# Sliding-window attention beside a gated MLP: P times V in two row tiles of 64 keys

## The chip, the cores and the metric

The kernel runs on one core of one Trainium2 chip. The metric is the device time of one execution in microseconds (us), as the median of several runs. The core's engines are TensorE (PE in the profile; PEld is its weight load), VectorE (DVE), ScalarE (ACT), GpSimd (POOL) and SyncE (SP), which issues the DMAs.

## What is computed

x has 2048 rows of 640. The result is x plus two branches of the same normalized x: causal attention in a sliding window, and a gated MLP. Cut from the reference:

```python
H = 32; Dh = D // H; W = 256                       # D = 640, so Dh = 20
q, k, v = split heads of (xn @ wqkv)
scores = einsum("bhqd,bhkd->bhqk", q, k) * (Dh ** -0.5)
mask = (idx[:, None] - idx[None, :] >= 0) & (idx[:, None] - idx[None, :] < W)
p = softmax(where(mask, scores, -1e9))
A = einsum("bhqk,bhkd->bhqd", p, v) -> (S, D) @ wo
B = (sigmoid(xn @ w_gate) * (xn @ w_up)) @ w_down  # F = 1536
return x + A + B                                   # xn = layernorm(x)
```

A query at position i sees the keys i - 255 to i: one diagonal piece, full pieces, and one oldest piece.

## The kernel before

The 2048 rows are worked in four chunks of 512 (`c` = 0 to 3). For each chunk the kernel normalizes x (`g_norms`; from chunk 1 on the reciprocal standard deviation `rstds` is made on POOL, L269 and L270, and the rows are scaled on DVE, L275), turns it so that features lie on partitions (`xnT`), and projects q, k and v (`proj_block` L302, `project_v` L330). q and k go through a scratch in DRAM (`st` to `sq`, `sk`, L310) and come back spread out (`spread`, L318), so that the 20 features of each head start at a partition divisible by 32. Four heads (`i` = 0 to 3) make a group; there are eight groups. v stays on chip with its keys on partitions: 21 columns per head, the last of them 0.5, which makes PV produce half the softmax denominator beside the output.

Attention goes in steps, listed by `steps_of` and run by `scores` (L485): a step fills one tile `ps` of 128 partitions x 4 heads x 512 columns in PSUM, ACT takes its exp into `pT` (L490), and POOL zeroes what the mask excludes (`affine_select`, here called a select, L493). A unit is 64 queries or 64 keys (`U`). In the step, partitions are 128 keys and columns are queries; the two halves of 64 keys are separate matmuls (`hf`), which write the two halves of the partitions. Each matmul has 20 rows and 64 columns of the array, at one of four row groups and two column halves. For chunks 1 to 3 a group has two wide steps (diagonal, full and oldest pieces, three selects each), and two groups share one full step, which has no select. Chunk 0 has two wide steps per group. That makes 16 steps in chunk 0 and 20 in each other chunk: 76.

`pv` (L519) then multiplies P by V for one group: each matmul takes 128 keys, the four heads write the four 32-partition strips of the accumulator `acc`, and the pieces of all steps accumulate. `finish_group` turns the accumulator on DVE (L529), `scale_group` divides (L537, L541) and turns it back to `oc` (L545).

The order of the work is written out by hand (`manual_schedule`): each engine runs its instructions in the order of the program. The main loop runs the 76 steps in order; after each step it pulls dense work out of a list (`Fill`): the projections of the next chunk, the MLP's gate and up matmuls (L412, L419, with tanh on ACT in L415 and the product `h` on DVE in L423), and the output rows (down projection L433, `wo` L440, row addition on DVE L444). How much is pulled is given by estimated costs, spread evenly over the steps up to a due time. P times V of a group is due one step after the last step of its pair (two in chunk 0), so that at that step both groups of the pair run `pv` one after the other, then the step's scores follow. Accumulators (`pg`, `pu`, `pqk`, `pv`, `y`, `acc`) share four PSUM slots in rotation; `ps` has one buffer (four banks), `pT` five.

Of the kernel before, what the change touches and what calls it, by code (L numbers as in the profile page):

```python
# [43 lines left out]
PTW = 10 * U  # L44

SPAN = 5


def wide_step(g, r, old):  # L60

    q = 2 * r
    if old:
        return dict(scores=[(g, 0, r, q, 5, 1), (g, 1, r, q + 1, 5, 2), (g, 0, r + 2, q + 4, 2, 6),
                            (g, 1, r - 2, q, 2, 0), (g, 0, r - 2, q, 1, 0), (g, 1, r + 2, q + 5, 1, 7)],
                    late=(1, 8, 2), diag=1, oldest=(0, 2),
                    pv=[(g, r, q, 5, 1), (g, r + 2, q + 4, 2, 6), (g, r, q + 5, 1, 9),
                        (g, r - 2, q, 2, 0, 8)])

    scores = [(g, 0, r, q, 5, 0), (g, 1, r, q, 6, 0)]  # L70
    if r == 0:
        scores += [(g, 0, 2, 4, 3, 5), (g, 1, 2, 5, 2, 6)]
        last = [(g, 2, 4, 3, 5)]
    else:
        scores += [(g, 0, 3, 6, 2, 5), (g, 1, 3, 7, 1, 6), (g, 0, 2, 7, 1, 7), (g, 1, 2, 7, 1, 7)]
        last = [(g, 3, 6, 2, 5), (g, 2, 7, 1, 7)]
    return dict(scores=scores, late=(5, 9, 1), diag=0, oldest=(4, 1),
                pv=[(g, r, q, 5, 0), (g, r, q + 5, 1, 9)] + last)


def full_step(gs):

    pieces = [(g, r, q, 2, 4 * n + col) for n, g in enumerate(gs) for r, q, col in ((-1, 0, 0), (2, 6, 2))]
    return dict(scores=[(g, hf, *rest) for g, *rest in pieces for hf in range(2)], pv=pieces)


def steps_of(c):
    if c == 0:
        return [wide_step(g, r, False) for g in range(NG) for r in range(2)]
    out = []  # L90
    for g in range(0, NG, 2):
        out += [wide_step(g + k, r, True) for k in range(2) for r in range(2)]
        out.append(full_step((g, g + 1)))
    return out
# [13 lines left out]
def kernel(  # L108
# [115 lines left out]
    def turn_wo():  # L224
        for i in range(HG):
            nc.sync.dma_start(out=wo_i[i].rearrange("(g d) n -> g d n", d=DH),
                              in_=A_wo.rearrange("(g i d) n -> i g d n", i=HG, d=DH)[i])
# [62 lines left out]


    qk = {}
    vt = {}

    def proj_block(w, c, m):

# [408 lines left out]
    for t, (c, _, step) in enumerate(todo):  # L705
        for piece in step["pv"]:
            ends[c, piece[0]] = t
# [96 lines left out]
```

## Time and profile before

| what | value |
|---|---|
| median of 3 runs | 312.26 us (312.17 to 312.5) |
| profiled execution, span from first to last instruction | 310.6 us |
| what lies around the span (median less span) | 1.66 us |
| granted TensorE clock, mean | 1.000 |
| instructions in the profile | 10139 |
| scores L485, PE | 1856 matmuls |
| P times V L519, PE | 1184 matmuls |
| selects L493, POOL | 192, 146.8 us busy |
| exp L490, ACT | 76, 142.7 us busy, 1878 ns each |

The profile lists busy time by engine, the span in 40 slices, the chain of work that ended last, groups of instructions by line, operation and tile, and the DMAs. A busy PE is not PE at its peak, as matmuls overlap; start times in the timeline show its pace.

### The profile page before, as it was taken

Reading aid. Unit: us, or ns where it says so; the run is one execution under the profiler, and the core shown is the slowest. Engines: PE = TensorE matmul, PEld = TensorE weight load, DVE = VectorE, ACT = ScalarE, POOL = GpSimd, SP = SyncE. Lnnn points to the kernel's source line nnn. Section 1 sums busy time; section 2 is a strip of 40 time slices with the busy share of each in tenths; the row PEclk is TensorE's granted clock in tenths of the full one; section 3 lists DMA queues with packets and bytes.
Section 4 is the critical chain, followed back from the end, with each engine's and each line's share of the span. In section 5 each row is a group of like instructions: output and inputs, shape, how many; then the busy total and the mean of one; then the engine's idle time right before and its main releaser. Section 6 shows DMA issues by size and latency. Waiting matters only on the chain.

```text
span 310.6 us, 10139 instructions
## 1 busy us (share of the span) xinstructions
PE 303.6 (98%) x4436; PEld 175.0 (56%) x4471; DVE 159.0 (51%) x313; ACT 192.5 (62%) x179; POOL 155.4 (50%) x239
## 2 busy tenths in 40 slices
PE   7999999999999999999999999999999999999996
PEld 3654444556557655644567665644546675454775
DVE  5533655639775154289826155272733526272423
ACT  6623878697763747787673647767585547768000
POOL 3000675676782827567382637546273846656000
PEclk9999999999999999999999999999999999999999
DMA  7997999765534153440035212450000220000302
GB/s 219 367 298 253 321 182 318 258 185 170 177 65 108 44 160 100 164 151 2 2 44 87 88 59 88 154 190 2 2 3 2 66 64 23 2 2 2 88 22 65
DMA packets 40301, 35.69 MB, mean 115 GB/s; under 512 B 10400, under 2 KB 39712, under 8 KB 40224
## 3 DMA queue, kind: packets, MB, share of 16 engines
q1 hardware_dynamic: 39392, 34.27, 37.6%
q10 hardware_dynamic: 864, 0.77, 0.9%
q8 instruction: 35, 0.57, 0.8%
q14 instruction: 10, 0.08, 0.1%
HBM read 23.63 MB, written 10.26 MB: 109 GB/s over the span
## 4 chain that ended last, share of the span: by engine, by line
PE 96%; issue 1%; DMA 1%; ACT 1%; DVE 0%; SPq 0%
PE y L433 17%; PE pu L419 17%; PE pg L412 17%; PE pqk L302 14%; PE ps L485 9%; PE pv L330 7%; PE y L440 7%; PE acc L519 7%; DMA xc<-in_A_x_dram 1%; PE pt L282 0%; ACT xn L614 0%; ACT xn L619 0%; DVE xn L625 0%; SPq L171 0%; ACT rstd L620 0%
## 5 line engine op out<-in xcount | busy, mean ns | idle before, releaser
L493 POOL TENSOR_SCALAR_AFFINE_SELECT pT<-pT 128x512 bf16<-128x512 bf16 (+2 forms) x192 | 146.8, 795 | 128.3 <-ACT pT L490 128.1
L490 ACT ACTIVATE pT<-ps 128x2048 bf16<-128x2048 f32 x76 | 142.7, 1878 | 64.3 <-PE ps L485 59.4
L423 DVE SCALAR_TENSOR_TENSOR h<-th,pu 128x512 bf16<-128x512 f32 x48 | 32.7, 683 | 58.2 <-PE pu L419 43.6
L419 PE MATMUL pu<-xnT,wu 128*128 128x512 bf16 x228 | 59.2, 380 | 0.7
L412 PE MATMUL pg<-xnT,wg 128*128 128x512 bf16 x226 | 58.0, 380 | 0.9 <-issue 0.5
L433 PE MATMUL y<-wd,h 128*128 128x320 bf16 (+2 forms) x396 | 57.0, 295 | 0.0
L302 PE MATMUL pqk<-xnT,wqkv 128*128 128x512 bf16 x191 | 45.7, 381 | 0.7 <-issue 0.2
L433 PEld LDWEIGHTS <-h 128*128 128x128 bf16 x396 | 36.6, 98 | 14.4
L415 ACT ACTIVATE th<-pg 128x512 f32<-128x512 f32 x48 | 28.6, 596 | 14.4 <-PE pg L412 14.0
L412 PEld LDWEIGHTS <-wg 128*128 128x128 bf16 x240 | 22.2, 98 | 25.2 <-issue 0.2
L419 PEld LDWEIGHTS <-wu 128*128 128x128 bf16 x240 | 21.9, 98 | 25.4 <-issue 0.6
L485 PEld LDWEIGHTS <-kT 20*64 20x64 bf16 x1856 | 20.6, 103 | 24.2 <-issue 22.3
L302 PEld LDWEIGHTS <-wqkv 128*128 128x128 bf16 x200 | 22.5, 119 | 18.4 <-issue 1.0
L529 DVE STREAM_TRANSPOSE t<-acc 128x512 f32<-128x512 f32 x32 | 21.8, 709 | 21.5 <-PE acc L519 21.2
L444 DVE SCALAR_TENSOR_TENSOR rows<-y,rows 128x320 bf16<-128x320 f32 x30 | 14.5, 490 | 35.2 <-PE y L440 30.2
L485 PE MATMUL ps<-qT,kT 20*64 20x128 bf16 (+4 forms) x1856 | 32.5, 239 | 0.0
L541 DVE TENSOR_TENSOR on<-t,rec 128x320 bf16<-128x320 f32 (+4 forms) x48 | 27.1, 565 | 1.1
L440 PE MATMUL y<-wo,oc 128*128 128x320 bf16 (+2 forms) x165 | 24.2, 295 | 0.0
L330 PE MATMUL pv<-wqkv,xnT 128*128 128x320 bf16 x160 | 23.7, 299 | 0.0
L519 PE MATMUL acc<-pT,v 128*32 128x128 bf16 (+3 forms) x1184 | 22.9, 231 | 0.0
L519 PEld LDWEIGHTS <-v 128*32 128x32 bf16 x1184 | 18.5, 97 | 7.5 <-issue 2.2
L440 PEld LDWEIGHTS <-oc 128*128 128x128 bf16 x165 | 15.5, 98 | 5.9
(45 smaller groups left out, 132.2 us busy)
## 6 DMA issues: line engine op xcount, KB each, us to landing
qT<-sq SPq DMA_DIRECT2D x7, 512.0 KB, 4.3
sq<-st SPq DMA_DIRECT2D x20, 128.0 KB, 3.6
sk<-st SPq DMA_DIRECT2D x20, 128.0 KB, 4.1
out_dram<-rows SPq DMA_DIRECT2D x15, 160.0 KB, 1.8
kT<-sk SPq DMA_DIRECT2D x4, 512.0 KB, 7.4
wg<-in_B_w_gate_dram SPq DMA_DIRECT2D x4, 480.0 KB, 7.1
wu<-in_B_w_up_dram SPq DMA_DIRECT2D x4, 480.0 KB, 6.1
xc<-in_A_x_dram SPq DMA_DIRECT2D x3, 640.0 KB, 5.5
```

The lines of the kernel that those rows point to most:

```text
L302: nc.tensor.matmul(ps, lhsT=wt[:, m, :], rhs=xnT[c][:, d, :], start=(d == 0), stop=(d == DC - 1))
L330: nc.tensor.matmul(ps[:, 0:HALF], lhsT=xnT[c][:, d, s * P:(s + 1) * P], rhs=wqkv[:, d, 2 * D + hf * HALF:2 * D + (hf + 1) * HALF], start=( ...
L412: nc.tensor.matmul(pg, lhsT=part(wg, d, f), rhs=xnT[c][:, d, :], start=(d == 0), stop=(d == DC - 1))
L415: nc.scalar.activation(out=th, in_=pg, func=TANH, scale=0.5)
L419: nc.tensor.matmul(pu, lhsT=part(wu, d, f), rhs=xnT[c][:, d, :], start=(d == 0), stop=(d == DC - 1))
L423: nc.vector.scalar_tensor_tensor(out=h, in0=th, scalar=1.0, in1=pu, op0=ADD, op1=MULT)
L433: nc.tensor.matmul(y[:, 0:cut[1] - cut[0]], lhsT=ht[c, f][:, s * P:(s + 1) * P], rhs=wd[:, f, cut[0]:cut[1]], start=(f == 0), stop=False)
L440: nc.tensor.matmul(y[:, 0:cut[1] - cut[0]], lhsT=oc[c, m][:, s * P:(s + 1) * P], rhs=wo[:, m, cut[0]:cut[1]], start=False, stop=(m == DC - 1))
L485: nc.tensor.matmul(ps[hf * U:(hf + 1) * U, i, col * U:(col + n) * U], lhsT=qk["k", kc, g // GH][32 * i:32 * i + DH, g % GH, key:key + U], ...
L490: nc.scalar.activation(out=pt[:, :, 0:CW], in_=ps, func=EXP, scale=SCALE)
L493: nc.gpsimd.affine_select(out=out, in_=in_, pattern=[[0, HG], [0, n], [sign, width]], compare_op=GE, fill=0.0, base=base, channel_multipli ...
L519: nc.tensor.matmul(acc[32 * i:32 * i + 32, q * U:(q + n) * U], lhsT=v[:, h * VW:h * VW + 32], rhs=cols[:, i, col:col + (n - 1) * by + 1:by ...
```

## The change

Two groups now share each step, one on each half of the partitions. `ps` and `pT` hold 64 keys on 64 partitions, for the first group of the pair on partitions 0 to 63 and for the second on 64 to 127. A step is a list of pieces `(u, q, n, col)`: the 64 keys of unit u, against n units of queries from unit q, in the columns from col. Chunk 0 has four steps per pair and the other chunks five, so there are 16 and 20 steps as before. Each piece is eight matmuls: two groups times four heads. Selects are made for each half of the partitions by itself: 264 instead of 192. For chunks 1 to 3 the five steps of a pair have 8, 4, 2, 2 and 2 of them.

`pv` runs both groups of the pair interleaved into two accumulators. Each matmul takes 64 keys in 64 rows of the array. Pieces are ordered by falling width. For half of the units the keys of V lie on the other half of the partitions, so each block of V gets a second tile `vx`, in which the halves are exchanged by two DMAs of 64 partitions x 347 elements (`swap_v`), issued on SP after the block's V is copied.

A pair is now made of group q of heads 0 to 15 and group q of heads 16 to 31. `spread` reads the scratch accordingly, two groups per DMA; `turn_wo` reorders wo accordingly, with eight DMAs instead of four; V is kept in two halves of 16 heads. The order of dense work is unchanged, and so are the places of the 76 steps and of the 16 places at which P times V runs.

```diff
...
+COLS = 8
+SPAN = 4
+VS = H // 2 * VW + 11
+def steps_of(c):
+    if c == 0:
+        plans = [([(6, 6, 2, 0), (0, 4, 1, 2), (1, 5, 1, 3), (7, 7, 1, 4), (2, 6, 1, 6), (3, 7, 1, 7)],
+                  (0,), (2, 3), [(6, 7, 1, 5)]),
+                 ([(4, 4, 4, 0), (5, 5, 3, 4)], (0,), (), [(5, 7, 1, 7)])]
     else:
+        plans = [([(6, 6, 2, 0), (0, 4, 1, 2), (1, 5, 1, 3), (7, 7, 1, 4), (2, 6, 1, 5), (3, 7, 1, 6), (-4, 0, 1, 7)],
+                  (0,), (2, 3, (5,)), []),
+                 ([(4, 4, 4, 0), (5, 5, 3, 4), (-3, 1, 1, 7)], (0,), ((7,),), []),
+                 ([(-1, 0, 4, 0), (-3, 0, 1, 4), (-2, 0, 3, 5)], (), (3,), [])]
+    plans += [([(u, u, 4, 0), (u + 1, u + 1, 4, 4)], (0,), (), []) for u in (0, 2)]
+    return [dict(pair=g, pv=pv, scores=pv + spare, diag=diag, oldest=oldest)
+            for g in range(0, NG, 2) for pv, diag, oldest, spare in plans]
...
     def turn_wo():
         for i in range(HG):
-            nc.sync.dma_start(out=wo_i[i].rearrange("(g d) n -> g d n", d=DH),
-                              in_=A_wo.rearrange("(g i d) n -> i g d n", i=HG, d=DH)[i])
+            for b in range(2):
+                nc.sync.dma_start(
+                    out=wo_i[i].rearrange("(q b d) n -> b q d n", b=2, d=DH)[b],
+                    in_=A_wo.rearrange("(b q i d) n -> i b q d n", b=2, i=HG, d=DH)[i, b])
...
-        src = scratch[w, c % 2].rearrange("(g p) s -> p g s", p=P)
-        nc.sync.dma_start(out=qk[w, c, half][:, first:first + g1 - g0, :], in_=src[:, g0:g1, :])
+        src = scratch[w, c % 2].rearrange("(b q p) s -> p q b s", b=2, p=P)
+        dst = qk[w, c, half][:, first:first + g1 - g0, :].rearrange("p (q b) s -> p q b s", b=2)
+        for k in range((g1 - g0) // 2):
+            nc.sync.dma_start(out=dst[:, k], in_=src[:, g0 // 2 + k])

     def new_v(c, s):
-        v = vp.tile([P, H * VW + 11], BF16, name="v")
+        v = vp.tile([P, 2, VS], BF16, name="v")
         vt[c * SBC + s] = v
-        nc.gpsimd.memset(v[:, 0:H * VW].rearrange("p (h d) -> p h d", d=VW)[:, :, DH:VW], 0.5)
-        nc.gpsimd.memset(v[:, H * VW:], 0.0)
+        nc.gpsimd.memset(v[:, :, 0:VS - 11].rearrange("p a (h d) -> p a h d", d=VW)[:, :, :, DH:VW], 0.5)
+        nc.gpsimd.memset(v[:, :, VS - 11:], 0.0)
+
+    def swap_v(c, s):
+
+        v, x = vt[c * SBC + s], vp.tile([P, VS], BF16, name="vx")
+        vx[c * SBC + s] = x
+        nc.sync.dma_start(out=x[0:U, :], in_=v[U:P, 0, :])
+        nc.sync.dma_start(out=x[U:P, :], in_=v[0:U, 1, :])
...
-        v3 = vt[c * SBC + s][:, 0:H * VW].rearrange("p (h d) -> p h d", d=VW)
-        copy(out=v3[:, hf * 16:(hf + 1) * 16, 0:DH],
+        v3 = vt[c * SBC + s][:, hf, 0:VS - 11].rearrange("p (h d) -> p h d", d=VW)
+        copy(out=v3[:, :, 0:DH],
              in_=ps[:, 0:HALF].rearrange("p (h d) -> p h d", d=DH))
...
             spread("q", c, 0, 2)
-            spread("k", c, 0, 1)
-            spread("k", c, 1, 3)
+            spread("k", c, 0, 2)
+            spread("k", c, 2, 4)
             spread("q", c, 2, 4)
-            spread("k", c, 3, 4)
+            for s in range(SBC):
+                swap_v(c, s)

     def g_v(c):
         for s in range(SBC):
             new_v(c, s)
             for hf in range(2):
                 proj_v(c, s, hf, nc.scalar.copy if hf else nc.vector.tensor_copy)
+            swap_v(c, s)
...
+        pt = pp.tile([P, HG, COLS * U], BF16, name="pT")
+        ps = ps_s.tile([P, HG, COLS * U], FP32, name="ps")
+        for u, q, n, col in step["scores"]:
+            kc, key = divmod(c * CW + u * U, CW)
+            for b in range(2):
+                g = step["pair"] + b
+                for i in range(HG):
+                    nc.tensor.matmul(
+                        ps[b * U:(b + 1) * U, i, col * U:(col + n) * U],
+                        lhsT=qk["k", kc, g // GH][32 * i:32 * i + DH, g % GH, key:key + U],
+                        rhs=qk["q", c, g // GH][32 * i:32 * i + DH, g % GH, q * U:(q + n) * U],
+                        start=True, stop=True)
+        nc.scalar.activation(out=pt, in_=ps, func=EXP, scale=SCALE)
+        cols = pt.rearrange("p h (n u) -> p h n u", u=U)
+        both = pt.rearrange("p h (a n u) -> p (h a) n u", n=SPAN, u=U)
+        for at, base, sign in [(x, 0, 1) for x in step["diag"]] + [(x, -1, -1) for x in step["oldest"]]:
+            for b in range(2):
+                rows = slice(b * U, (b + 1) * U)
+                live = cols[rows, :, at[0], :] if isinstance(at, tuple) else both[rows, :, at, :]
+                nc.gpsimd.affine_select(out=live, in_=live, pattern=[[0, live.shape[1]], [sign, U]],
+                                        compare_op=GE, fill=0.0, base=base, channel_multiplier=-sign)
         return pt

+    def pv(c, pair, made):
+        accs = [ps_d.tile([P, CW], FP32, name="acc", tag="d") for _ in range(2)]
+        flat = sorted(((piece, pt) for step, pt in made for piece in step["pv"]), key=lambda x: -x[0][2])
+        for k, ((u, q, n, col), pt) in enumerate(flat):
+            block = (c * CW + u * U) // P
+            for b in range(2):
+                rows = slice(b * U, (b + 1) * U)
+                v = vt[block][rows, b, :] if u % 2 == b else vx[block][rows, :]
+                for i in range(HG):
+                    h = (pair // 2 * HG + i) * VW
+                    nc.tensor.matmul(
+                        accs[b][32 * i:32 * i + 32, q * U:(q + n) * U],
+                        lhsT=v[:, h:h + 32], rhs=pt[rows, i, col * U:(col + n) * U],
+                        start=(k == 0), stop=(k == len(flat) - 1), skip_group_check=True)
+        for b in range(2):
+            finish_group(c, pair + b, accs[b])

...
+    ends = {(c, step["pair"]): t for t, (c, _, step) in enumerate(todo)}
+    due = {t + (1 if c else 2): (c, pair) for (c, pair), t in ends.items()}
+    cuts = [(ends[n, NG - 2] + 2 + n, f"out{n}") for n in range(NCH - 1)] + [(len(todo), None)]
...
+            n, pair = due[t]
+            fill.hurry = pair == NG - 2
+            pv(n, pair, parts.pop((n, pair)))
+            if pair == NG - 2:
+                fill.shut.discard(f"out{n}")
+        parts.setdefault((c, step["pair"]), []).append((step, scores(c, step)))
```

## The prediction

> **What bounds the kernel now.** I read the page from the top: busy shares, slices, the chain. Then groups with shapes kept apart, then timelines of two places.
>
> ```profile
> PE 303.6 (98%) x4436; PEld 175.0 (56%) x4471; DVE 159.0 (51%) x313; ACT 192.5 (62%) x179; POOL 155.4 (50%) x239
> ...
> PE   7999999999999999999999999999999999999996
> ...
> PEclk9999999999999999999999999999999999999999
> ...
> q8 instruction: 35, 0.57, 0.8%
> ...
> PE 96%; issue 1%; DMA 1%; ACT 1%; DVE 0%; SPq 0%
> PE y L433 17%; PE pu L419 17%; PE pg L412 17%; PE pqk L302 14%; PE ps L485 9%; PE pv L330 7%; PE y L440 7%; PE acc L519 7%; DMA xc<-in_A_x_dram 1%; PE pt L282 0%; ACT xn L614 0%; ACT xn L619 0%; DVE xn L625 0%; SPq L171 0%; ACT rstd L620 0%
> ```
>
> TensorE works from the second slice to the last at the full clock and is 96% of the chain. No other engine is near its limit, so time moves only if TensorE's stream gets shorter or is made to wait. Of that stream the change touches scores (L485, 9%) and PV (L519, 7% of 310.6, 21.7 us); the order of everything else on PE, DVE and ACT is the same in both programs.
>
> The stream's pace comes from start times. Dense matmuls of 512 columns start 216 ns apart, of 320 columns 136 ns: columns / 2.4 + 2.5 ns. The scores' and PV's small matmuls start 3 to 5 ns apart when they lie on different tiles of the array, and the next wave on the same tiles follows after the same columns / 2.4 + 2.5 (136 ns for 320, 56 for 128, 28 for 64). So a burst costs the columns per tile, plus 2.5 ns a wave, plus some 0.1 us at each change of tile shape: in one PV burst 80 matmuls take 1.44 us to the next matmul's start, against 3072 / 2.4 + 20 x 2.5 = 1.33.
>
> ```profile
> 109.62 0.43 PE L485 MATMUL ps<-qT,kT 20*64 20x128 bf16 x32
> 109.98 2.35 PE L302 MATMUL pqk<-xnT,wqkv 128*128 128x512 bf16 x10
> 112.27 1.51 PE L519 MATMUL acc<-pT,v 128*32 128x320 bf16 x80
> 113.71 0.43 PE L485 MATMUL ps<-qT,kT 20*64 20x320 bf16 x24
> ```
> ```profile
> 110.21 1.88 ACT L490 ACTIVATE pT<-ps 128x2048 bf16<-128x2048 f32 x1 [1.80 <-PE ps L485]
> ```
>
> These two timelines (start, length) show the second pair of chunk 1: the pair's last score step, its exp, which ends at 112.09, and PV, which starts 0.18 us later.
>
> **The change, part by part. PV** had 1184 matmuls, four tiles of 128 keys side by side; it gets 2016, eight tiles of 64 keys. A pair of groups in chunks 1 to 3 streamed 48 units of 64 columns (3072) in 20 waves; now 40 units (2560) in 17 waves: 1.33 to 1.11 us, saving 0.22. In chunk 0, 36 units in 14 waves become 30 in 12: 0.995 to 0.83, saving 0.165. 12 x 0.22 + 4 x 0.165 = 3.3 us. The first wave of a burst now has eight starts ahead of the next wave, not four: 13 ns x 16 = 0.2 less. **PV: -3.1 us**, if eight 64-row tiles run side by side. The scores' eight tiles (four row groups, two column halves) do so in this trace.
>
> **Scores** go from 1856 matmuls to 2080, but each of the 76 steps still streams 512 columns per tile; waves per pair go from 16 to 17, in chunk 0 from 10 to 14: 28 x 2.5 ns = 0.07 us. Exp still does 2048 elements 76 times (1.88 us). Nothing.
>
> **The wait on POOL** is the price.
>
> ```profile
> L493 POOL TENSOR_SCALAR_AFFINE_SELECT pT<-pT 128x1024 bf16<-128x1024 bf16 x64 | 70.6, 1103 | 0.0
> L493 POOL TENSOR_SCALAR_AFFINE_SELECT pT<-pT 128x512 bf16<-128x512 bf16 x96 | 63.7, 687 | 85.5 <-ACT pT L490 85.4
> ...
> L493 POOL TENSOR_SCALAR_AFFINE_SELECT pT<-pT 128x256 bf16<-128x256 bf16 x32 | 15.4, 500 | 42.7 <-ACT pT L490 42.7
> ```
>
> Here a pair's last step in chunks 1 to 3 (the full step) has no select: PV needs only its exp. Afterwards the last step is diagonal (units 2 and 3) with two selects, each 512 elements on 64 partitions, and PV's fifth wave waits for both. No row shows 64 partitions: if time goes with elements per partition it is 687 ns, if with all elements the 500 ns row is the nearest. I take 687, since all present selects cover 128 partitions and follow elements per partition; at 500 lies the other end. In the trace a select starts 0.07 after its exp, and back-to-back selects overlap by 0.05. So PV may go on at exp end + 0.07 + 2 x 0.687 - 0.05 + 0.07 = exp end + 1.46. Four waves of 256 columns come before (4 x 0.109, plus the spread of starts: 0.475). A burst stalls by 0.99 us less its lead, the time from exp end to PV start. The leads in this trace, for the twelve pairs of chunks 1 to 3: 1.80, 0.18, 0.43, 1.29, 1.04, 1.52, 0.71, 1.23, 0.50, 0.44, 0.21, 3.47 us. Six stall: 0.81 + 0.56 + 0.28 + 0.49 + 0.55 + 0.78 = **+3.5 us**. With the 500 ns row the limit falls to 0.61: 0.43 + 0.18 + 0.11 + 0.17 + 0.40 = 1.3; with selects stretched by 10% it rises to 1.13 and the sum to 4.4. PE runs in order, so behind the waiting matmul everything waits, and the next pair finds its own lead unchanged: the stalls add up. In chunk 0 leads are 2.7 us (PV comes two steps later): none. All selects together go from 149.7 to 216 x 0.687 + 48 x 0.5 = 172 us: POOL stays under 60%.
>
> **rstds behind the selects.** A first step of chunk 1 has eight selects (4.5 us back to back) where three stood.
>
> ```profile
> 84.22 1.11 POOL L270 TENSOR_TENSOR rstds<-rstds,neghalf 128x4 f32<-128x4 f32 x1
> ```
> ```profile
> 87.01 2.84 DVE L275 TENSOR_SCALAR xn<-xc,mvs,rstds 128x640 bf16<-128x640 bf16 x4
> 89.77 0.67 DVE L423 SCALAR_TENSOR_TENSOR h<-th,pu 128x512 bf16<-128x512 f32 x1
> 90.36 0.48 DVE L444 SCALAR_TENSOR_TENSOR rows<-y,rows 128x320 bf16<-128x320 f32 x1
> ```
> ```profile
> 89.46 1.53 PE L440 MATMUL y<-wo,oc 128*128 128x320 bf16 x10
> 90.83 0.98 PE L433 MATMUL y<-wd,h 128*128 128x320 bf16 x6
> ```
>
> That exp ends at 81.54, so rstds would end at 81.6 + 4.5 + 0.23 + 1.1 = 87.45 instead of 85.33. DVE reaches the normalization at 87.01 and would wait 0.45; h and the row addition behind it slip as much, and the y of L433 at 90.83, four accumulators later, takes the slot which that addition frees at 90.84. **+0.45 us**, between 0 (the slot frees a little earlier) and 0.5. The other two norms come out no later than before or have slack of microseconds.
>
> **DMA.** SyncE issues 30 more DMAs (32 swaps of 44 KB; spreads and the turning of wo regrouped), some 0.4 us each by the rows of its queue. Chunk 1 is the tight place: kT was issued at 75.10, when the stored k had landed, and is first read at 79.03. Two swaps now go ahead of it; their v is copied by 72.85 and its pads set by 74.74, so kT slips to about 75.6 and lands 2.8 us later (the median for its size), at 78.4. Cover 0.6 us; without it, up to 1 us once. In chunk 0 eight swaps precede wg's second half: issue 29.06 to about 31.8, landing near 36, first read 38.12. wo, wd and the later chunks have several microseconds. Nothing. PSUM: both accumulators are now needed at PV's start; the slot of the second was free 0.39 us or more ahead in all 16 bursts. Nothing.
>
> **The sum:** -3.1 + 0.1 + 3.5 + 0.45 = +0.9 us on a span of 310.6. The median of the runs, 312.26, is 1.66 us above the span, which the change does not touch: 312.26 + 0.9 = **313.1 us**.
>
> **Feeding TensorE** is the unknown. The densest stretch of this trace is a PV burst with the score step behind it: 104 weight loads and matmuls in 1.68 us, 16 ns a pair, without any slip. Afterwards it is 136 + 56 = 192 pairs in 1.6 us, 8 ns a pair. Faster pairs (3.3 ns) show only in runs of up to 32. If the instruction stream gave no more than 16.2 ns a pair, 192 pairs would take 3.1 us, 1.5 more in twelve bursts, and 152 pairs in chunk 0 1.2 more in four: +23 us. At no limit it is zero. I take zero, the nearer row being the 3.3 ns runs with the same tile count, and keep the other end. In the page's instruction queue, TensorE's code comes in 35 packets of 16 KB, and in the trace each took 0.9 to 1.5 us, one per 256 instructions. A burst of 384 instructions in 1.6 us uses one and a half such packets.
>
> [...]
>
> **Rivals.** (B) *The selects are hidden*: half the partitions cost the 500 ns row or less, and the rstds slip does not reach PE. -3.0 + 1.3 or less gives 309.2 to 310.6; I price it 310.2. It decides from selects under about 0.60 us each. For it: nothing shows a 64-partition select. Against: the three forms follow elements per partition. (C) *The feed limits*: 317 to 336. For it: twice the density ever shown. Against: no slip anywhere now. (D) *The change doesn't do what it says*: the two row halves run one after the other. Then PV costs 2 x 1.11 and 2 x 0.83: +0.89 x 12 + 0.66 x 4 = 13.3, stalls 1.1 as the four waves cover more, rstds 0.45: 327. Against: the scores' row groups overlap now.
>
> **Chances.** Forecast (311.7 to 314.5) 0.45; B 0.25; C 0.22; D 0.08. A measurement of this kernel tells 0.2% (0.6 us) from no change: 311.6 to 312.9 counts as the same. Of the forecast 0.18 lies there and 0.27 above; of B 0.23 is faster and 0.02 the same. Faster 0.23, same 0.20, slower 0.57. The range goes from all gain and no loss (-3.1, 309.1) up to 322, which leaves out D and half of C.
>
> **What would show it.** PV bursts of 1.22 us to the next start in the last pair, but about 2 us in the second pair of chunk 1, with TensorE waiting for pT of POOL inside L499 (the new PV line); selects of about 0.69 us; 172 us for all; a first step's eight selects and rstds ending near 87 us. Selects near 0.5 us, or no waits inside PV, make me wrong downward; bursts above 1.3 us without a wait on POOL make the feed or the row halves the cause.

## The result and the profile after

The changed kernel takes 336.6 us (median of 4 runs, 333.4 to 340.9), the kernel before 312.2 beside it (4 runs): 1.074 times as long (interval 1.069 to 1.080). Forecast were 313.1 us in a range of 309.1 to 322.0. The direction was the likeliest one of the prediction, the size was not: 24 us were lost where 0.9 had been added up. Its runs also differ by 2%, those of the kernel before by 0.2%; the median takes in the slowest run, 340.9 us, which the ratio leaves out as slow.

The page of the changed kernel, its profiled execution of 333.8 us:

```profile
PE 318.3 (95%) x5527; PEld 181.0 (54%) x5527; DVE 156.7 (47%) x313; ACT 192.4 (58%) x179; POOL 173.4 (52%) x311
...
PE   7999979999999999789999999979999999979996
...
PEclk9999998999999999979999999979999999999999
...
q8 instruction: 43, 0.70, 0.9%
...
PE 88%; ACT 4%; issue 3%; POOL 2%; DMA 1%; DVE 0%; SPq 0%; POOLq 0%
...
L473 PE MATMUL ps<-qT,kT 20*64 20x64 bf16 (+3 forms) x2080 | 37.7, 237 | 9.0 <-issue 8.9
...
L473 PEld LDWEIGHTS <-kT 20*64 20x64 bf16 x2080 | 21.6, 104 | 33.4 <-issue 32.3
```

The same two groups on the page of the kernel before:

```profile
L485 PEld LDWEIGHTS <-kT 20*64 20x64 bf16 x1856 | 20.6, 103 | 24.2 <-issue 22.3
...
L485 PE MATMUL ps<-qT,kT 20*64 20x128 bf16 (+4 forms) x1856 | 32.5, 239 | 0.0
```

TensorE's row has holes now (7 and 8 where 9s stood), its clock dips in three slices, and 9.0 us of idle time stand ahead of the scores' matmuls (L473, L485 before) where there was none, put down to "issue": TensorE waits for nothing that the profile shows. (Of the idle time ahead of their weight loads most stood there before.) TensorE's code comes in 43 packets in place of 35. By start times, TensorE's stream divides as follows (us; the last column is the repaired kernel E17 below):

| part of TensorE's stream | before | after | after less before | E17 |
|---|---|---|---|---|
| dense matmuls | 257.2 | 262.0 | +4.8 | 257.7 |
| scores | 28.0 | 41.6 | +13.6 | 28.1 |
| P times V | 21.8 | 26.6 | +4.8 | 19.2 |

Most of the loss is in the scores, whose streamed columns did not change. The timeline of the changed kernel at the seventh pair of chunks 1 to 3 (start, length, instruction, and in brackets the idle time before it with its cause) shows how:

```profile
215.91 0.22 PE L499 MATMUL acc<-pT,v 64*32 64x64 bf16 x4
216.06 0.42 PE L473 MATMUL ps<-qT,kT 20*64 20x128 bf16 x24
218.88 0.33 PE L473 MATMUL ps<-qT,kT 20*64 20x64 bf16 x32 [2.40 <-issue]
219.15 2.25 PE L399 MATMUL pg<-xnT,wg 128*128 128x512 bf16 x5
```

P times V (L499) ends, 24 of the 56 score matmuls run, and then nothing starts for 2.6 us, although kT, qT and ps are ready. There are six such holes, of 2.47, 0.56, 0.44, 2.49, 2.61 and 1.79 us, 10.4 us in all. Every one lies at the same place of TensorE's instruction stream: counted from 0 over all of its records (matmuls, weight loads and 25 others, mostly waits for semaphores), the first instruction after the hole is number 193 plus a multiple of 256, the start of a line in what follows. In the DMA records the 16 KB packet of code that belongs to this hole runs from 216.49 to 217.44, inside it. Taking packets and lines in order, this holds for the whole trace: of 42 line ends TensorE reached six before the packet of the next line had landed or less than 1 us after, and these are the six holes; it reached the other 36 at least 1.19 us after the landing and shows no hole there. No line began less than 1.25 us after its packet had landed. And no packet came long ahead: a line's packet started between 2.6 us before TensorE entered the line ahead of it and 3.7 us after.

Two more things are to be seen in timelines. After the first waves of a burst the small matmuls no longer start 3 ns apart but every 8.33 ns, one pair of weight load and matmul; the twelve bursts of 136 take 1.54 us to the next start where nothing else holds them, and the 56 scores behind them 0.60 in place of 0.37. And the clock drops behind a long hole. Here are the stretches of the hole at 140.2 us, of what follows it, and of the time after that (stretch; length and busy time of each engine; granted clock; DMA):

```profile
140.00:142.70 2.70, 0.41 (x44) 0.25 (x30) 1.31 (x2) 0.00 (x0) 0.00 (x0) 1.00 0.91 282
142.70:147.50 4.80, 4.79 (x65) 1.94 (x66) 3.08 (x7) 2.94 (x3) 2.18 (x3) 0.65 0.23 62
147.50:149.00 1.50, 1.50 (x8) 0.69 (x7) 0.88 (x2) 1.41 (x1) 1.40 (x3) 0.98 0.00 0
```

For 2.5 to 3.4 us the dense matmuls start 427 ns apart in place of 216. This happens behind the three holes of 2.47 us and more, and nowhere else in this trace; it makes the 4.8 us of the dense part.

### The profile page after: what moved, and what is told of

Its sections match the earlier page's. It is cut to its first block, busy times and chain, and to the rows that moved or that the text cites. A ratio compares the mean times of both kernels' runs of the same rounds, so it can differ in the third digit from the quotient of the medians.

```text
span 333.8 us, 12408 instructions
## 1 busy us (share of the span) xinstructions
PE 318.3 (95%) x5527; PEld 181.0 (54%) x5527; DVE 156.7 (47%) x313; ACT 192.4 (58%) x179; POOL 173.4 (52%) x311
## 4 chain that ended last, share of the span: by engine, by line
PE 88%; ACT 4%; issue 3%; POOL 2%; DMA 1%; DVE 0%; SPq 0%; POOLq 0%
PE pu L406 16%; PE pg L399 16%; PE y L420 15%; PE pqk L278 13%; PE ps L473 10%; PE y L427 7%; PE acc L499 6%; PE pv L315 5%; ACT pT L478 3%; POOL pT L485 2%; DMA xc<-in_A_x_dram 1%; PE pt L257 0%; ACT xn L595 0%; ACT xn L600 0%; DVE xn L606 0%
## 5 line engine op out<-in xcount | busy, mean ns | idle before, releaser
L485 POOL TENSOR_SCALAR_AFFINE_SELECT pT<-pT 64x512 bf16<-64x512 bf16 (+1 forms) x264 | 164.1, 622 | 137.0 <-ACT pT L478 124.7
L399 PE MATMUL pg<-xnT,wg 128*128 128x512 bf16 x240 | 62.1, 391 | 0.0
L406 PE MATMUL pu<-xnT,wu 128*128 128x512 bf16 x240 | 62.0, 390 | 0.0
L473 PE MATMUL ps<-qT,kT 20*64 20x64 bf16 (+3 forms) x2080 | 37.7, 237 | 9.0 <-issue 8.9
L473 PEld LDWEIGHTS <-kT 20*64 20x64 bf16 x2080 | 21.6, 104 | 33.4 <-issue 32.3
L510 DVE STREAM_TRANSPOSE t<-acc 128x512 f32<-128x512 f32 x32 | 21.1, 696 | 35.2 <-PE acc L499 35.2
L499 PE MATMUL acc<-pT,vx 64*32 64x64 bf16 (+3 forms) x1008 | 24.4, 230 | 1.6 <-POOL pT L485 1.6
L499 PE MATMUL acc<-pT,v 64*32 64x64 bf16 (+3 forms) x1008 | 25.5, 230 | 0.0
L522 DVE TENSOR_TENSOR on<-t,rec 128x320 bf16<-128x320 f32 (+4 forms) x48 | 24.6, 512 | 1.1
L499 PEld LDWEIGHTS <-v 64*32 64x32 bf16 x1008 | 21.6, 91 | 6.0 <-issue 1.7
```

The costliest lines, as they stand in the source:

```text
L399: nc.tensor.matmul(pg, lhsT=part(wg, d, f), rhs=xnT[c][:, d, :], start=(d == 0), stop=(d == DC - 1))
L406: nc.tensor.matmul(pu, lhsT=part(wu, d, f), rhs=xnT[c][:, d, :], start=(d == 0), stop=(d == DC - 1))
L473: nc.tensor.matmul(ps[b * U:(b + 1) * U, i, col * U:(col + n) * U], lhsT=qk["k", kc, g // GH][32 * i:32 * i + DH, g % GH, key:key + U], rh ...
L485: nc.gpsimd.affine_select(out=live, in_=live, pattern=[[0, live.shape[1]], [sign, U]], compare_op=GE, fill=0.0, base=base, channel_multipl ...
L499: nc.tensor.matmul(accs[b][32 * i:32 * i + 32, q * U:(q + n) * U], lhsT=v[:, h:h + 32], rhs=pt[rows, i, col * U:(col + n) * U], start=(k = ...
```

## The experiments

The theory after this reading: **the number of small instructions** is what costs. TensorE's code comes in lines of 256 instructions (43 packets for 11079 records), one ahead (by the times of the packets just given), and a burst of 272 + 112 instructions runs through a line before the next has come (refill); between such stalls pairs come in at 8.33 ns (feed). The rivals: the row tiles of 64 keys are slow by themselves; the selects and the waits on POOL are the loss; the DMAs are. "Before" is always the kernel before on the same chip, within 0.3 us of 312.1.

**E1, the same work at other places of the instruction stream.**

```diff
-    for n in (6, 4):
+    for n in (48, 32):
...
-            nc.tensor.matmul(ps, lhsT=ones[:, 0:P], rhs=ones, start=(k == 0), stop=(k == n - 1))
+            nc.tensor.matmul(ps[0:32, 0:U], lhsT=ones[:, 0:32], rhs=ones[:, 0:U],
+                             start=(k == 0), stop=(k == n - 1))
```

> The changed kernel, with its ten warm-up matmuls of 512 columns replaced by eighty of 64 columns; nothing else moves, so all later instructions of TensorE stand 140 places later in its stream. Theory (refill): TensorE's code comes in lines of 256 instructions, one line ahead, and a line is usable only some 4 us after the one before it is entered, so a stall falls where two line ends fall into P times V and the scores behind it (384 instructions in 2.1 us). The line ends now fall at other places: from the order of the program and the pace in the changed kernel's trace I work out 17 to 19 us of such stalls in place of 8 to 11, at six to eight pairs in place of four, and about 1.7 us more for each long stall for the drop of the clock behind it: 343 to 355 us, with the stalls again every 256 instructions, 140 places off. Rivals (the row tiles, the selects or the DMAs cost the time): the same 334 to 341 as the changed kernel, and stalls at the same matmuls.

344.2 us, ratio 1.104 (1.096 to 1.111). The second pair of chunk 1, which had no refill stall in the changed kernel, has one of 2.2 us now:

```profile
121.74 0.64 PE L474 MATMUL ps<-qT,kT 20*64 20x128 bf16 x53
124.39 0.26 PE L474 MATMUL ps<-qT,kT 20*64 20x64 bf16 x3 [2.01 <-issue]
```

There are eight stalls in chunks 1 to 3, 14.1 us in all (10.4 without the shift). Counted by weight loads, of which this trace lacks none, all eight lie at number 193 of a line again, to one, and so at other matmuls than in the changed kernel. The sum was put too high at 17 to 19. Of the 5.6 us between the two traces 3.7 are stalls; 1.9 are a wait for kT at 81 us that the changed kernel does not have. That stalls come and go with the place of the same work in the stream refutes the rivals as the cause of the holes.

**E2 and E10, P times V one step later.** In E2 the space for the sixth pT comes from two of the six st buffers, in E10 from th (bf16 in place of f32).

```diff
-    pp = pool("pp", 5)
+    pp = pool("pp", 6)
-    due = {t + (1 if c else 2): (c, pair) for (c, pair), t in ends.items()}
+    due = {t + 2: (c, pair) for (c, pair), t in ends.items()}
```

> The changed kernel with P times V of chunks 1 to 3 one step later (two steps after the pair's last, as in chunk 0), six buffers for pT and four for st. Theory: the waits on POOL inside P times V (3.0 us in five bursts of the changed kernel's trace) are gone, the pace of 8.3 ns a pair stays, and the refill stalls stay at 6 to 10 us but at other pairs: 328 to 336 us. Rival (selects are the main cost): back to 311 to 316 us. Rival (row tiles cost it): 333 to 337.

> e2_late without its cut in st: the changed kernel's pieces, P times V of chunks 1 to 3 one step later, six buffers of pT and of st, th in bf16. It shows what instructions alone cost, without waits on POOL. Theory: POOL's 3.0 us and e2's st waits (some 3 us in chunk 0 and 1) gone, refill stalls of 6 to 10 us, the 8.3 ns pace (some 8 us) and clock drops (2 to 5 us) stay: 326 to 333 us. Rival (selects and waits on them are the main loss): below 318 us.

E2 333.6 us, ratio 1.067 (1.061 to 1.074); E10 329.7 us, 1.057 (1.052 to 1.061). In both no wait on POOL is left inside P times V, ten of the twelve bursts of E10 take 1.54 us, and its refill stalls add up to 10 us. P times V falls from 26.6 to 23.5 us in E10. So the waits on POOL were some 3 us of the loss, and not its main part.

**E4, the burst broken up.** On top of E2, dense work within and behind P times V.

```diff
+            if k in (6, 12) and fill.parts and fill.parts[0][0][:2] in ("gu", "qk"):
+                between.append(fill.one())
...
+            credit -= 2000 - fill.pull(2000)
         parts.setdefault((c, step["pair"]), []).append((step, scores(c, step)))
```

> As e2_late, and P times V is issued in three portions of 96, 96 and 80 instructions with ten dense instructions (a projection, gate or up tile of 1.1 us) between them, and 2.2 us of dense work before the scores that follow; where output rows or V are due between, P times V stays in one piece. Work and instructions are the same. Theory (refill and feed): 256 small instructions now take about 4 us, so the stalls fall from 8 to 11 us to 3 to 5, the clock drops with them, and the queue of TensorE is full again before the scores; two more changes of tile shape per burst cost 0.2 us: 316 to 326 us. Rival (row tiles of 64 keys or their weight loads cost the time wherever they stand): no better than e2_late, or 2 us worse by the changes of shape.

348.2 us, ratio 1.114 (1.110 to 1.118): the time missed the expectation, and the experiment says little about the theory. The refill stalls did shrink, to 3.1 us in five places. But six score steps wait 13.8 us for the exp of the step before. At 70 us it is 3.5 us, as ACT had stood 9.0 us before that exp for one of the four st buffers. At 91 and 94 us and three times at the end the dense work pulled ahead was missing: score steps follow each other with nothing between.

**E5, the kernel before with more instructions and nothing else of the change.**

```diff
         flat = [(pt, *piece[1:]) for step, pt in parts for piece in step["pv"] if piece[0] == g]
+        flat = [(pt, r, q + at, n, col + at * (step[0] if step else 1), *step)
+                for pt, r, q, m, col, *step in flat
+                for at, n in (((0, m),) if m == 1 else ((0, (m + 1) // 2), ((m + 1) // 2, m // 2)))]
```

> The kernel before, with each matmul of P times V of two or more units split into two of half the columns: 2080 matmuls in place of 1184, the same streamed columns, 128-key tiles, selects, DMAs and steps as before. Theory (the number of small instructions is the cause): bursts of 288 + 112 instructions in chunks 1 to 3 stall for refill as the changed kernel's do; worked out from the order and the pace 9 to 12 us in about six pairs, and 2 to 6 us of clock drops: 320 to 332 us. Rival (row tiles, selects or DMAs of the change): 312 to 314 us, as the split only adds 2.5 ns a wave, 0.5 us in all.

326.6 us, ratio 1.045 (1.039 to 1.051). Its timeline at the first pair of chunk 1:

```profile
97.16 1.57 PE L522 MATMUL acc<-pT,v 128*32 128x192 bf16 x144
98.66 0.32 PE L485 MATMUL ps<-qT,kT 20*64 20x320 bf16 x1
99.71 0.42 PE L485 MATMUL ps<-qT,kT 20*64 20x320 bf16 x23 [0.73 <-issue]
```

P times V itself takes 1.50 us to the next start (1.44 before; at 8.33 ns its 144 pairs would take 1.20, so its columns are the bound), and one score matmul later the hole follows. Eight such holes sum up to 11.8 us, as worked out (9 to 12); counted by weight loads, all lie within two of number 193 of a line, and TensorE goes on 1.2 to 1.5 us after a packet has landed. The clock stayed at 1.0 in this execution, the fastest of the four (324.5 us), which the expectation had not said; the other three show 0.990 to 0.995. So 14.5 us can be lost without any row tile, swap or new select.

**E6 and E7, fewer instructions in the same row tiles.** Each unit of keys meets its five units of queries in one piece where a step's columns allow it: 12 pieces per pair in place of 17, with the same columns; the pieces of the last step come last. E7 also has P times V one step later, with E2's edit and the st of chunk 0 in h's buffers.

```diff
+        plans = [([(0, 0, 5, 0), (-2, 0, 3, 5)], (0,), (4, 7), []),
+                 ([(1, 1, 5, 0), (5, 5, 3, 5)], (0, 5), (4,), []),
+                 ([(2, 2, 5, 0), (-3, 0, 2, 5), (7, 7, 1, 7)], (0, 7), (4, 6), []),
+                 ([(3, 3, 5, 0), (6, 6, 2, 5), (-4, 0, 1, 7)], (0, 5), (4, 7), []),
+                 ([(-1, 0, 4, 0), (4, 4, 4, 4)], (4,), (3,), [])]
...
+                live = cols[rows, :, at, :]
```

> The changed kernel with its pieces grouped anew: each unit of 64 keys meets its (up to) five units of queries in one piece where the eight columns of a step allow it, so that a pair of chunks 1 to 3 has 12 pieces in five steps (17 in the changed kernel), chunk 0 has 9 (12). P times V stays in two row tiles of 64 keys, with the same 2560 streamed columns per pair; 192 instructions in place of 272, and 32 for the scores behind it in place of 112. Selects are of 256 elements, 32 per pair; the last step has four. Theory (number of small instructions): no two line ends fall into one burst any more, so no refill stall, and eight tiles of 320 columns (136 ns) are longer than the 67 ns that eight pairs take to come in, so P times V takes 1.2 us and no clock drops: -3.5 us against the kernel before, plus 1 to 3 us of waits on POOL for the last step's four selects (4 x 0.412): 309 to 312 us. Rival (row tiles, 64-key weight loads, DMAs or selects cost the time, not the count of instructions): 330 to 337 us, as the tiles, DMAs and the select time stay.

> As e6_regroup, with P times V of chunks 1 to 3 one step later (six buffers of pT; four of st, and the st of chunk 0 in the buffers of h). Theory: the waits on POOL inside P times V go too: 308 to 310.5 us, below the kernel before. Rival: as in e6_regroup, 328 us or more.

E6 333.2 us, ratio 1.068 (1.065 to 1.070); E7 322.3 us, 1.033 (1.032 to 1.035). Both miss their times, and E6 by as much as the rival would have it. But the traces say that the counted mechanism is gone: no hole at a line end in either, and scores of 27.3 us in E6. E6 loses in P times V (37.4 us in place of 19): its selects of 256 elements take 201 us on POOL (164 in the changed kernel), POOL falls behind, and P times V waits for it in nearly every burst, up to 1.4 us at a time, several times. In E7 that is gone (P times V 20.5 us), and another wait stands where chunk 1 is projected, on ACT and then on TensorE:

```profile
68.31 0.58 ACT L285 CAST st<-pqk 128x512 bf16<-128x512 f32 x1 [4.80 <-DMA sq<-st]
```
```profile
70.73 0.65 PE L474 MATMUL ps<-qT,kT 20*64 20x320 bf16 x16 [4.35 <-ACT pT L479]
```

ACT waits for one of the st buffers, of which I had taken two away; the exp behind it in ACT's order is late, and TensorE needs ps.

**E8, the instructions put back.** E7 with each piece of P times V split as in E5, everything else kept.

> As e7_regroup_late, with each matmul of P times V of two or more units split into two: 176 per pair in place of 96 in chunks 1 to 3, the same columns, tiles, selects, steps and DMAs. Theory: bursts of 352 + 32 instructions bring the refill stalls back, worked out as 13 to 17 us, and P times V takes 1.47 us by the pace of 8.33 ns a pair (+4 us in all), and the clock drops add 2 to 6: 326 to 336 us. Rival (the gain of e7_regroup_late, if any, comes from the selects or the steps' order): within 1 us of e7_regroup_late.

337.8 us, ratio 1.080 (1.075 to 1.084), above the expected range by 1.8 us: some 15 us more than E7, by the split alone.

**E9, all six st buffers.** As E7, but all st use their own six buffers again; the space comes from th in bf16.

```diff
-            th = tp.tile([P, CW], FP32, name="th")
+            th = tp.tile([P, CW], BF16, name="th")
```

> As e7_regroup_late, but with all six buffers of st; the space comes from th, the output of tanh, held in bf16 in place of f32. In e7_regroup_late the trace shows ACT waiting 4.80 us for the st buffer of a DMA, TensorE then 4.42 us for exp, a clock drop behind it, and no refill stall. Theory (number of small instructions is what the changed kernel lost by; e7's remaining loss is the st buffers): without that wait TensorE's stream is dense work as before (257.2 us), P times V 20.5 us as in e7 (21.8 before), scores 27.9 - 4.4 = 23.5 (28.0 before): 312.0 - 5.8 = 306 us, say 305 to 309, below the kernel before. Rival (row tiles or the two DMAs per block of V keep a cost that e7 hides among its waits): 316 us or more.

316.5 us, ratio 1.014 (1.012 to 1.016). That is 6 us better than E7 but 7 above the expectation, at the rival's number. The place of the loss is narrow: set against the same dense matmuls of the kernel before, the stream is 0.4 us late at 57 us, 6.2 late at 93 us, and 4.9 at its end.

**E11, wide and narrow pieces by turns; E12, half of the masks on DVE.**

```diff
+        flat = [flat[k // 2 if k % 2 == 0 else -1 - k // 2] for k in range(len(flat))]
```
```diff
+                nc.vector.tensor_tensor(out=live, in0=live, in1=old.to_broadcast([P, HG, U]), op=MULT)
```

> As e9_regroup_late6, but the pieces of P times V go wide and narrow by turns (5, 1, 5, 1, 5, 2, 5, 2, 3, 3 units, then the last step's 4, 4) in place of falling width. In e9 the trace shows the four waves of 320 columns at 136 ns, and from the second wave of 64 columns on one matmul every 8.33 ns up to the end, so that the two waves of 256 columns come 118 ns after each other with their starts spread over 58 ns; the burst takes 1.35 us to the next start. Theory (pairs come in at 8.33 ns, and TensorE's queue fills up only while a wave takes longer than its eight pairs): with a wide wave behind each narrow one the queue never drains: 12 waves, 2560 / 2.4 + 12 x 2.5 = 1.10 and 0.12 for the change of shape, 1.22 us, so 12 x 0.13 and some 0.1 in each burst of chunk 0: 314.2 to 315.2 us (e9: 316.5). Rival (narrow waves are slow in 64-row tiles by themselves, whatever stands before them): 316 to 317 us.

> As e11_interleave; the mask of the oldest pieces is a product with a constant on DVE, one step after the scores (112 of 256 elements on all 128 partitions, in place of 224 selects on POOL), and the swaps of V are issued behind the spreads of q and k. In e9 POOL runs selects back to back from 65 to 82 us, P times V, the exp and the scores of chunk 0's end wait some 2.3 us for them, and kT comes 2.2 us late since its DMA stands behind the swaps, whose V waits for the pads that POOL writes behind the selects. Theory: these 4.5 to 5 us and a clock drop behind them go: 308 to 311 us, below the kernel before. Rival (row tiles keep a cost that no experiment so far has taken away): 313 us or more.

E11 315.3 us, ratio 1.010 (1.009 to 1.012): a burst takes 1.26 us in place of 1.35 (1.22 expected), with nothing but the order changed: that fits the feed as the cause, though not all of the 0.13 us comes back. E12 313.1 us, 1.002 (1.000 to 1.004), and its own mechanism is not what the trace shows: POOL fell from 210 to 121 us, and the waits near 69 to 81 us stayed. That trace is of the slowest of twelve runs (315.3 us), and the median is 2.2 us below E11; which of E12's two edits, the masks or kT ahead of the swaps, brought this is not shown. The trace names another carrier. In E12, ACT and SP's queue:

```profile
68.62 0.59 ACT L285 CAST st<-pqk 128x512 bf16<-128x512 f32 x1 [2.70 <-DMA sq<-st]
```
```profile
48.55 6.07 SPq L201 DMA_DIRECT2D wo_i<-in_A_wo_dram  x8
...
61.41 3.79 SPq L287 DMA_DIRECT2D sq<-st  x4
```

and the same two steps of SP's queue in the kernel before:

```profile
44.74 2.81 SPq L226 DMA_DIRECT2D wo_i<-in_A_wo_dram  x4
...
56.98 5.56 SPq L310 DMA_DIRECT2D sq<-st  x4
```

SP issues one DMA after the other, each swap in 0.5 to 0.6 us. Eight swaps (28.3 to 33.3 us) and four more DMAs for wo make it 4.4 us late where the projections' st must leave.

**E13 to E17, the queue.** E13 is E12, E14 is E11 (with kT ahead of the swaps), both with chunk 0's swaps on ACT's queue and wo in four DMAs; E15 is E14 with wo in eight again; E16 adds three warm-up matmuls; E17 puts the swaps on POOL's queue. The cut is E17's place for them.

```diff
-            for s in range(SBC):
-                swap_v(c, s)
...
+    for s in range(SBC):
+        swap_v(0, s, nc.gpsimd)
     for _ in g_qk(0):
```

> As e12_masks_dve; the eight swaps of chunk 0's V are issued on ACT's queue before the first projection (ACT is idle there for 5.2 us), and the turning of wo takes four DMAs again in place of eight. e12_masks_dve refuted its own mechanism: with POOL down from 210 to 121 us busy the waits near 69 to 81 us stayed. Its trace shows another carrier, SP's queue: the eight swaps hold SP from 28.3 to 33.3 us, the wo DMAs take 6.1 us where the kernel before takes 2.8, the transposes end at 47.9 in place of 44.1, and the projections' st leave late (ACT waits 2.70 us for a buffer of st, TensorE then for accumulators and exp, and kT lands 2.2 us late). Theory (queue): without these eight swaps and four DMAs ahead, SP is at or ahead of the kernel before; the 0.8 + 0.5 + 0.8 + 2.2 us of gaps go, and about 1 us for the clock: 307 to 310 us, below the kernel before. Rival (POOL or the row tiles keep it): 312 us or more.

> As e13_queue, but with all selects on POOL as in e11_interleave. Theory (queue alone was the cause of the remaining loss): within 1 us of e13_queue, 307 to 311 us. Rival (POOL's 210 us matter as well): 2 us or more above e13_queue, with waits on POOL pT or rstds in the trace.

> As e14_queue_pool, but the turning of wo takes its eight DMAs again; only the eight swaps of chunk 0 stay on ACT's queue. e13 and e14 were slower because of my four wo DMAs: their rows of one head run together, the transfer goes at 47 GB/s over few DMA engines, and the wd DMAs behind them hold SP for 14.6 us (4.4 in e12_masks_dve), so the test of the queue told nothing. Theory (queue): SP reaches the projections' st about 4.8 us earlier than in e12_masks_dve, so the waits for st (2.7 us on ACT), for accumulators and exp near 69 to 72 us and most of the 2.2 us for kT go: 308 to 311 us, below the kernel before. Rival (the waits there have another cause): 313 to 316 us, as e11_interleave and e12_masks_dve.

> As e15_swaps_act, with three more warm-up matmuls of 512 columns ahead of the first transposes (13 in place of 10). In e15's trace no wait near 69 to 82 us is left, but its stream is 1.95 us late from the start on: TensorE idles 1.11 us before the first transposes (0.45 in the kernel before), and the first ten projections of V take 2.74 us in place of 1.60, at half the clock. Theory: with the gap filled they run at the full clock and 1.5 to 1.9 us come back: 310.2 to 311 us, 0.4 to 0.6% below the kernel before; the stream holds P times V of 19.2 us against 21.8 and otherwise the work of before. Rival (the late start is another thing, a later x): 312 us as e15.

> As e16_warm, with the eight swaps of chunk 0 on POOL's queue, where POOL has no select before 32 us. In e16_warm the late start is gone (its stream is 0.7 us ahead of the kernel before at 24 us), but ACT holds the swaps from 14.8 to 21.2 us, the copies of st behind them wait 6.65 us, and the first scores wait 1.8 us for kT at 32.4 us. Theory (what is left is only where the swaps are queued): these 2 us go: 309.8 to 311 us, 0.4 to 0.8% below the kernel before, near the 2.6 us that P times V saves. Rival (the swaps cost the same wherever they are queued, as transfers among the first weights): 312 us.

E13 319.8 us (1.023, 1.020 to 1.026) and E14 320.1 (1.024, 1.020 to 1.027): equal, so POOL's load does not matter there, but both worse. My four DMAs for wo moved at 47 GB/s, and SP's queue stood behind them:

```profile
50.48 14.57 SPq L194 DMA_DIRECT2D wd<-in_B_w_down_dram  x5
```

E15 312.1 us (1.001, 0.999 to 1.002): the waits for st, exp and kT near 69 to 82 us are gone, which shows that SP's queue made them. E16 312.4 us (1.000, 0.998 to 1.002): the late start of E15 is gone, but the first kT was late instead, since ACT held the swaps; no gain. **E17 310.2 us, ratio 0.993 (0.991 to 0.995)**: faster than both kernels, by 0.7% than the kernel before. On its page, and at a burst of P times V:

```profile
PE 301.2 (98%) x4313; PEld 167.9 (54%) x4346; DVE 150.8 (49%) x313; ACT 192.4 (62%) x179; POOL 214.2 (69%) x535
```
```profile
132.56 0.32 PE L499 MATMUL acc<-pT,v 64*32 64x320 bf16 x4
...
133.60 0.29 PE L499 MATMUL acc<-pT,vx 64*32 64x256 bf16 x4
133.82 0.42 PE L472 MATMUL ps<-qT,kT 20*64 20x320 bf16 x16
134.18 0.39 PE L405 MATMUL pu<-xnT,wu 128*128 128x512 bf16 x1
```

The burst that began at 132.56 ends at the scores' start at 133.82, 1.26 us later (1.44 before), and the scores follow without a hole.

**E18, the side edits alone.** The kernel before with th in bf16 and three more warm-up matmuls.

> The kernel before with the two side edits of e17_swaps_pool that have nothing to do with P times V: th in bf16 and three more warm-up matmuls. Theory (e17's gain of 1.8 us comes from P times V in row tiles): 311.7 to 312.6 us, as the kernel before, since th bounds nothing there and the first transposes wait for x. Rival (the side edits carry e17's gain): 310 to 311 us.

312.3 us, ratio 1.000 (0.998 to 1.001): neither carries E17's gain. The table above has it in P times V alone (2.6 us less; the dense matmuls take 0.5 us more). P times V one step later was not tried in the kernel before, but its bursts of chunks 1 to 3 all take 1.44 or 1.45 us and show no wait that this could save.

## Why the prediction was wrong

**The step that failed** is the feed of TensorE: "At no limit it is zero. I take zero, the nearer row being the 3.3 ns runs with the same tile count, and keep the other end." The other end was +23 us, and that is what came, though in other parts than "16 ns a pair": 10.4 us of refill stalls, 8.0 us of feed at 8.33 ns a pair (P times V 12 x (1.54 - 1.22) and 1.0 in chunk 0, scores 3.2), and 4.8 us of clock drops behind the stalls. The waits on POOL and some small ones (3.4 us) and the saving of P times V about cancel, as forecast. Rival C (317 to 336 us) described it, at a chance of 0.22; for its lower end, 317 us, no row or run shows a term, and what the runs showed in its place are the 10.4 us of refill stalls. The wrong choice was the row: runs of up to 32 pairs at 3.3 ns did not show the pace of a long burst: in those of 136 one pair came every 8.33 ns behind the first waves. That the short runs are faster because a queue had filled up while a dense matmul ran is my guess: E11's gain by order alone (1.26 us a burst in place of 1.35) fits it, and no trace shows it. The prediction had the count that mattered in its hands, 384 instructions in 1.6 us at one packet per 256, and did not price a packet of 0.9 to 1.5 us against it. And "no slip anywhere now" was not so. Behind the very burst that it shows, at 114.75 us, the kernel before has two projection matmuls 0.56 us apart in place of 0.22, within one of number 193 of a line, and goes on 1.50 us after a packet has landed.

The runs side with the lines as the cause of the stalls: these stand a multiple of 256 instructions apart, E5 and E8 bring the loss back at will by more instructions alone (14.5 and some 15 us), and in the changed kernel no line's packet started more than 2.6 us before TensorE entered the line ahead of it. Nor did TensorE go on as soon as a packet had landed: behind the six holes it went on 1.25 to 1.56 us later, at 218.88 us 1.4 us later.

**P times V -3.1 us**: right as a mechanism. Eight tiles of 64 rows run side by side (rival D is refuted: waves of 256 columns start 110 ns apart), and in E17 the part is 2.6 us shorter than before. In the changed kernel it could not be seen, as 26.6 us stood in its place.

**Scores +0.1 us**: wrong by 13.5 us, by the failed step; the columns were counted and the instructions were not.

**The wait on POOL +3.5 us**: right in place and in size. All six forecast bursts wait at the fifth wave: over the 1.54 us of the others they take 0.75, 0.50, 0.22, 0.49, 0.52 and 0.77 us (3.25; forecast 0.81, 0.56, 0.28, 0.49, 0.55 and 0.78, 3.5). In the third of them, at 214.66 us, the second select ends at 214.95 and the next wave starts at 215.00. The first of them in the timeline of the changed kernel:

```profile
119.41 0.45 PE L499 MATMUL acc<-pT,v 64*32 64x256 bf16 x8
120.28 0.30 PE L499 MATMUL acc<-pT,vx 64*32 64x256 bf16 x8 [0.43 <-POOL pT L485]
```

A select of 512 elements on 64 partitions takes 668 ns (687 taken), one of 256 takes 412 (500 taken): elements per partition count, so rival B fell. E2 and E10 agree with 3 us.

**rstds +0.45 us**: the DVE waited for rstds twice, 2.6 us in all, but TensorE shows no wait behind it that the kernel before lacks. The term cannot be told from zero.

**DMA "Nothing"**: true in the changed kernel, whose trace shows no wait for kT, though SP issues 46 more DMAs there and not 30 (184 against 138), and the eight swaps of chunk 0 take 0.6 us each and not 0.4. It seems that TensorE's own lateness hid them: E1, the same program with its stalls elsewhere, waits 1.9 us for kT. In E11 and E12, with the instructions repaired, the same DMAs cost: E15, which takes eight swaps off SP and puts kT ahead of the others, is 3.2 us below E11, and E17 2.1 us below E16 by the queue alone. "Cover 0.6 us; without it, up to 1 us once" had looked at kT and at wg, and not at the st buffers behind 4.4 us of SP's queue. **PSUM "Nothing"**: no wait showed.

Why the changed kernel's runs differ by 2% is not settled. That the moment at which a packet comes decides over stalls of up to 2.6 us and the clock behind them would fit, but was not tried.

## What to carry to other kernels

Where a change splits matmuls into smaller ones, count the instructions of each burst beside its columns: here bursts that reached a new line of 256 before its packet was in, and long runs of pairs that stream for less than 8.33 ns each, cost more than the columns saved (10.4 us of stalls and 8.0 of feed, against 3.1 forecast as saved and 2.6 seen in E17). A fast run of a few dozen instructions in a trace is not a rate; look for the longest run at that pace (here 3.3 ns held for up to 32 pairs, and 8.33 ns was the pace in the bursts of 136). A DMA added to a busy queue is priced by what is queued behind it, and its cover is only as good as the lateness of the engine that hides it: when the main loss is repaired, price it again (no wait in the changed kernel, but 3.2 us between E11 and E15).

## What the runs showed of the hardware

- TensorE's instructions came in lines of 256: packets of 16 KB on the instruction queue, 43 for 11079 recorded instructions in the changed kernel, each 0.9 to 2.1 us, and all six holes at number 193 plus a multiple of 256. No line began there less than 1.25 us after its packet had landed; a line end reached too early for that was a stall of up to 2.6 us. Speed alone did not make one: a line passed in 1.34 us, at 196 us, brought none, as the next packet had landed before.
- The steady rate of small matmuls was one pair of weight load and matmul per 8.33 ns in the changed kernel, whether for scores (20 rows) or for P times V (64 rows).
- In the changed kernel TensorE ran for about 3.4 us at half of its clock behind each of the holes of 2.47 to 2.61 us (mean 0.53 from 144 to 147 us), and not behind 1.79 us. The length does not decide alone: in E1 the clock stayed at 1.00 behind a hole of 2.44 us at 181.6 us and fell to 0.51 behind one of 1.92 us at 279.9.
- Issuing a swap of V held its queue for about 0.5 to 0.6 us, on SP (E12), ACT (E15) and POOL (E17) alike; over all DMAs on SP in E12 the median was 0.53. In E13 the wo DMAs, whose rows of a head ran together, moved at 47 GB/s.
